# A DiT block on one core: LN2's second token tile turned by VectorE and moved by DMA, ten fc1 tiles per small token tile, two weight blocks loaded earlier, a P V remainder in quarters

## The chip, the core and the metric

The kernel runs on one core of one Trainium2 chip. The metric is the device time in microseconds. Before the change it is 241.34 us (median of 3 runs, 241.32 to 241.39). A core has TensorE (matrix multiplication into PSUM), VectorE, ScalarE (activation functions, copies), GpSimd and SyncE (which here only issues DMAs); each runs its own instructions strictly in order, and they wait for each other on semaphores.

## The reference

One block of a diffusion transformer: B = 2, N = 256 tokens, D = 1152, 2 heads of 576, hidden width F = 4608, all inputs bfloat16.

```python
mod = (_silu(c) @ w_mod).reshape(B, 6, 1, D)
shift_a, scale_a, gate_a, shift_m, scale_m, gate_m = [mod[:, i] for i in range(6)]
h = _layernorm(x) * (1 + scale_a) + shift_a
qkv = (h @ wqkv).reshape(B, N, 3, H, Dh)
...
attn = _softmax(einsum('bqhd,bkhd->bhqk', q, k) * Dh ** (-0.5))
a = einsum('bhqk,bkhd->bqhd', attn, v).reshape(B, N, D) @ wo
x = x + gate_a * a
h2 = _layernorm(x) * (1 + scale_m) + shift_m
return x + gate_m * (_gelu(h2 @ w_fc1) @ w_fc2)
```

## The kernel before

The 512 tokens are four tiles of 128 (t = 0 to 3; two tiles per batch element b = t // 2). D is nine chunks of 128 (kt), F is 36 tiles of 128 (f). Weights live in SBUF regions that are used again and again; all of SBUF is one tensor, `arena`, all of PSUM one tensor, `psum`, so these two names stand in nearly every line of the profile.

The kernel is written as a list of units (one operation each, or a group of matmuls). TensorE and SyncE run theirs in the order of the program text. For the other engines a planner orders the units by the length of what hangs on them, with a cost for each unit; `S.in_order` (lines 1317 to 1333) fixes the order of the units that it names. Waits are worked out from the memory that units read and write. PSUM has eight banks; `acc_bank()` hands out those in `acc` in turn.

What matters here begins with the attention output, P V: `pv(b, h)` makes eight chunks of 128 features; the 128 features left over (64 of each head, since 576 = 4 x 128 + 64) are made by `pv_halves()` (line 1127), two matmuls of 64 columns side by side in the array (`tile_position`), four such pairs. Just ahead of it, `rows()` makes the modulation vectors with matmuls that have 2 columns of weights, four side by side.

Then `wo_tile(t)` (line 1161) for t = 0 to 3: three PSUM tiles of 384 features, nine matmuls each. For each one VectorE multiplies by the gate (`wo_t1`, line 1173), GpSimd adds x (`wo_x1`, line 1174); then LN2's statistics on VectorE (`bn_ln2`, `aggr`, `veps`, lines 751 to 754), rstd and the negative mean times rstd on GpSimd (`rstd`, `negm2`, `nmr2`), and the normalized tile on ScalarE (`xn2_t`, line 1180).

fc1 needs the normalized tile transposed (features in partitions). Two ways are in the kernel:

- `xn2_T(t)`, used for t = 1, inside `wo_tile(3)` after its first third: nine transposes on TensorE (line 706), then nine scalings out of PSUM (`h2T_1_kt`: four on VectorE, five on ScalarE).
- `xn2_turn(t)` (one VectorE transpose of 32 x 32 blocks, `h2turn_t`, line 1206) with `xn2_move(t)` (four DMAs from SBUF to SBUF on SyncE's queue, `mv_h2_t_a`, which put the blocks in their partitions; then nine scalings in place, `h2T_t_kt`, lines 1216 on ScalarE and 1219 on VectorE), used for t = 0, 2, 3. `TURNED` says where the turned tile is put before it is moved.

fc1 follows (`fc1_tile(f, tok0, ntok)`): nine matmuls for each f and token range, then a GELU on ScalarE (line 1229) into `GT[f]`. w_fc1 comes in nine blocks of four f each (`wfc1_load(q)`, 1152 KB), into four buffers; blocks 0 and 1 are loaded during attention, 2 and 3 into the region of wv and w_mod's shift part, behind tile 0's moves on SyncE's queue. The order of fc1: f = 0 to 4 on tile 1, f = 0 to 4 on tile 0, f = 5 to 14 on tiles 0 and 1 together (256 tokens), f = 0 to 14 on tiles 2 and 3, then f = 15 to 35 on all 512 tokens. During that, `ld_gm` brings the last part of w_mod (2592 KB), from which VectorE works out the MLP's gate (`mlp_gate`), and SyncE loads w_fc1's and w_fc2's other blocks. fc2 ends the kernel.

SyncE's order in this part: blocks 0 and 1, the second gate (`ld_g1`), tile 0's moves, blocks 2 and 3, the moves of tiles 2 and 3, `ld_gm`, then blocks 4 to 8 of w_fc1 and the four of w_fc2.

Of the kernel before, what the change touches and what calls it, by code (L numbers as in the profile page):

```python
# [508 lines left out]
KT = 9  # L509
# [4 lines left out]
SCALE = DH ** -0.5  # L514
CH = 384
NCH = 3
F0 = 15
KC = 5
KG = 6
NG = 9  # L520
# [3 lines left out]
def c_mm(n):  # L524
    return max(n / 2.4 + 2.5, 27.0)
# [26 lines left out]
def build_kernel(nc, x, c, wqkv, wo, w_mod, w_fc1, w_fc2, out):  # L552
# [5 lines left out]
    with (  # L558
# [14 lines left out]
        def ps16(bank, c0=0, n=1024):  # L573
            v = psum[:, bank * 512: (bank + 1) * 512].bitcast(BF16)
            return v[:, c0:c0 + n]
# [111 lines left out]
        def dve(cost, fn, reads, writes, name):  # L687
            return S.op("dve", cost, fn, reads=reads, writes=writes, name=name)

        def act(cost, fn, reads, writes, name):  # L690
            return S.op("act", cost, fn, reads=reads, writes=writes, name=name)
# [10 lines left out]
        def mm(o, l, r, st, sp, **kw):  # L702
            S.instr(lambda e: e.matmul(o, lhsT=l, rhs=r, start=st, stop=sp, **kw), reads=[l, r], writes=[o])  # L703

        def tr(o, i_, idn):
            S.instr(lambda e: e.transpose(o, i_, idn), reads=[i_, idn], writes=[o])  # L706
# [420 lines left out]
        def pv_halves():  # L1127
            S.unit("pe", 4 * c_mm(256) + 100.0, "PV_halves")
            for b in range(2):
                for kjt in range(2):  # L1130
                    for h in range(2):
                        f0 = 512 + 64 * h
                        mm(psum[64 * h:64 * h + 64, b * 256:b * 256 + 256], V[:, 2 * b + kjt, f0:f0 + 64],
                           PTS[b * 2 + h][:, kjt], b == 0 and kjt == 0, b == 1 and kjt == 1, skip_group_check=True,
                           tile_position=(0, 64 * h))
            copy_on("act", OT[:, 4, :], ps32(0), 512, False, "OT_ev_4")

        def pv(b, h):
# [11 lines left out]
                copy_on(eng, OT[:, g:g + 2, tok], src, 512, False, "OT_ev%d_%d" % (b, g))  # L1150

        act(1500, lambda e: e.activation(out=SUMS[:, 0:1], in_=NHALF, func=ACTF.Gelu_apprx_tanh), [NHALF], [SUMS[:, 0:1]], "gelu_tab")
        acc = [2, 3, 4, 6, 5, 7]
        acc_rr = [0]

        def acc_bank():
# [1 line left out]
            acc_rr[0] += 1  # L1158
            return b

        def wo_tile(t, before={}):
            b = t // 2
            for ci in range(NCH):
                if ci in before:
                    before[ci]()
                S.unit("pe", KT * c_mm(CH), "wo_%d_%d" % (t, ci))
                o = ps32(acc_bank(), 0, CH)
                for g in range(KT):
                    mm(o, OT[:, g, t * 128:(t + 1) * 128], WO[:, g, ci * CH:(ci + 1) * CH], g == 0, g == KT - 1)
                ga = GA[b][:, ci * CH:(ci + 1) * CH]  # L1170
                x1c = X1[:, t, ci * CH:(ci + 1) * CH]
                xs = X[:, t, ci * CH:(ci + 1) * CH]
                dve(550, lambda e, o=o, ga=ga, x1c=x1c: e.tensor_tensor(out=x1c, in0=o, in1=ga, op=ALU.mult), [o, ga], [x1c], "wo_t1_%d_%d" % (t, ci))  # L1173
                S.op("pool", 930, lambda e, xs=xs, x1c=x1c: e.tensor_tensor(out=x1c, in0=x1c, in1=xs, op=ALU.add),  # L1174
                     reads=[x1c, xs], writes=[x1c], name="wo_x1_%d_%d" % (t, ci))
            rs, nm, m, xn2, x1 = RSTD2[:, t:t + 1], NMR2[:, t:t + 1], MV2[:, t, 0:1], XN2[t], X1[:, t, :]
            ln_stats_dve(x1, [X1[:, t, ci * CH:(ci + 1) * CH] for ci in range(NCH)], BN2[:, t, :], MV2[:, t, :], rs, "ln2_%d" % t)
            pool(200, lambda e: e.tensor_scalar(out=nm, in0=m, scalar1=-1.0, scalar2=None, op0=ALU.mult), [m], [nm], "negm2_%d" % t)
            pool(200, lambda e: e.tensor_tensor(out=nm, in0=nm, in1=rs, op=ALU.mult), [nm, rs], [nm], "nmr2_%d" % t)  # L1179
            act(1344, lambda e: e.activation(out=xn2, in_=x1, func=ACTF.Identity, scale=rs, bias=nm), [x1, rs, nm], [xn2], "xn2_%d" % t)  # L1180

        last_h2T = [None]

        def xn2_T(t):
            b = t // 2
            xn2 = XN2[t]
            S.unit("pe", KT * c_mm(128), "xn2T_%d" % t)
            hi, lo = ((7, 6), (1, 0))[t % 2]
            slot = [ps16(hi, kt * 128, 128) if kt < 4 else ps16(lo, (kt - 4) * 128, 128) for kt in range(KT)]
            for kt in range(KT):  # L1190
                tr(slot[kt], xn2[:, kt * 128:(kt + 1) * 128], IDENT)
            for kt in range(KT):
                o, dst = slot[kt].rearrange("p (g i) -> p g i", i=32), H2T[:, kt, 4 * t:4 * t + 4, :]
                s1, s2 = SC1M[:, kt * 2 + b:kt * 2 + b + 1], SHM[:, kt * 32 + b:kt * 32 + b + 1]
                if kt < 4:
                    last_h2T[0] = dve(335, lambda e, o=o, dst=dst, s1=s1, s2=s2: e.tensor_scalar(out=dst, in0=o, scalar1=s1, scalar2=s2, op0=ALU.mult, op1=ALU.add),
                        [o, s1, s2], [dst], "h2T_%d_%d" % (t, kt))
                else:
                    act(440, lambda e, o=o, dst=dst, s1=s1, s2=s2: e.activation(out=dst, in_=o, func=ACTF.Identity, scale=s1, bias=s2),
                        [o, s1, s2], [dst], "h2T_%d_%d" % (t, kt))  # L1200

        TURNED = {0: H2F[3], 2: XN2[0], 3: XN2[1]}

        def xn2_turn(t):
            src, flat = XN2[t].rearrange("p (k x c) -> p c k x", k=KT, c=4), TURNED[t]
# [2 lines left out]
        def xn2_move(t):  # L1208
            b, b0 = t // 2, 0
            for a in range(4):  # L1210
                dma(H2F[t][:, 288 * a:288 * a + 288], TURNED[t][32 * a:32 * a + 32, :], P * 576, "mv_h2_%d_%d" % (t, a), run=576)
            for kt in range(KT):
                dst = H2T[:, kt, 4 * t:4 * t + 4, :]
                s1, s2 = SC1M[:, kt * 2 + b:kt * 2 + b + 1], SHM[:, kt * 32 + b:kt * 32 + b + 1]
                if kt % 3 if t == 0 else kt % 3 == 2:
                    act(330, lambda e, dst=dst, s1=s1, s2=s2: e.activation(out=dst, in_=dst, func=ACTF.Identity, scale=s1, bias=s2),  # L1216
                        [dst, s1, s2], [dst], "h2T_%d_%d" % (t, kt))
                    continue
                last_h2T[0] = dve(220, lambda e, dst=dst, s1=s1, s2=s2: e.tensor_scalar(out=dst, in0=dst, scalar1=s1, scalar2=s2, op0=ALU.mult, op1=ALU.add),  # L1219
                    [dst, s1, s2], [dst], "h2T_%d_%d" % (t, kt))  # L1220
# [46 lines left out]
        def wfc2_load(q):  # L1267
            dma(WFC2[:, 9 * q:9 * q + 9, :], wfc2_v[:, 9 * q:9 * q + 9, :], 9 * P * D * 2, "ld_wfc2_%d" % q, run=2304)

        wo_tile(0)  # L1270
        xn2_turn(0)
        xn2_move(0)
        wfc1_load(2)
        wfc1_load(3)
        wo_tile(1)
        wo_tile(2)
        xn2_turn(2)
        wo_tile(3, {1: lambda: xn2_T(1)})
        xn2_turn(3)
        xn2_move(2)  # L1280
        xn2_move(3)
        dma(WGM, wmod_v[:, :, 5 * D:6 * D], D * D * 2, "ld_gm", run=2304)
        for tok0 in (128, 0):
            for f in range(0, 5):
                fc1_tile(f, tok0, 128)
        for f in range(5, F0):
            fc1_tile(f, 0, 256)
        mlp_gate(last_h2T[0])
        for f in range(F0):
# [11 lines left out]
        for t in range(4):  # L1301
# [4 lines left out]
            for (c0, c1) in pieces:  # L1306
# [3 lines left out]
                for j in range(JT):  # L1310
# [13 lines left out]
        S.in_order("act", ["sexp_0_0", "sexp_0_1", "qk_ev8", "spn_0_0", "spn_0_1", "v_ev0_0", "sexp_2_0", "sexp_2_1", "sexp_1_0", "sexp_1_1", "v_ev0_1",  # L1324
                           "spn_2_0", "spn_2_1", "spn_1_0", "spn_1_1", "v_ev0_2", "sexp_3_0", "sexp_3_1", "v_ev1_0", "spn_3_0", "spn_3_1", "v_ev1_1", "v_ev1_2"])
        S.in_order("act", ["OT_ev0_0", "OT_ev0_2", "OT_ev1_0", "OT_ev1_2", "OT_ev_4", "OT_ev0_5", "OT_ev1_5", "gelu_tab", "xn2_0"])
        S.in_order("pool", ["wo_x1_0_0", "wo_x1_0_1", "wo_x1_0_2", "wo_x1_1_0", "rstd_ln2_0", "nmr2_0", "wo_x1_1_1", "wo_x1_1_2", "wo_x1_2_0", "rstd_ln2_1", "nmr2_1", "wo_x1_2_1", "wo_x1_2_2",
                            "wo_x1_3_0", "rstd_ln2_2", "nmr2_2", "wo_x1_3_1", "wo_x1_3_2", "rstd_ln2_3"])
        S.in_order("dve", ["wo_t1_0_0", "wo_t1_0_1", "bn_ln2_0_0", "wo_t1_0_2", "bn_ln2_0_1", "wo_t1_1_0", "bn_ln2_0_2", "aggr_ln2_0", "veps_ln2_0", "wo_t1_1_1",
                           "bn_ln2_1_0", "wo_t1_1_2", "bn_ln2_1_1", "wo_t1_2_0", "bn_ln2_1_2", "aggr_ln2_1", "veps_ln2_1", "h2turn_0", "wo_t1_2_1", "bn_ln2_2_0", "wo_t1_2_2", "bn_ln2_2_1",  # L1330
                           "wo_t1_3_0", "h2T_1_0", "h2T_1_1", "h2T_1_2", "h2T_1_3", "bn_ln2_2_2", "aggr_ln2_2", "veps_ln2_2", "wo_t1_3_1", "wo_t1_3_2", "h2T_0_0", "h2T_0_3", "h2T_0_6",
                           "bn_ln2_3_0", "bn_ln2_3_1", "bn_ln2_3_2", "aggr_ln2_3", "veps_ln2_3", "h2turn_2", "h2turn_3"])
        S.in_order("act", ["xn2_0", "xn2_1", "h2T_1_4", "h2T_1_5", "h2T_1_6", "h2T_1_7", "h2T_1_8", "h2T_0_1", "h2T_0_2", "h2T_0_4", "h2T_0_5", "h2T_0_7", "h2T_0_8", "gelu_0_128", "xn2_2"])
        S.schedule()
        if VERBOSE:
            S.report()
# [50 lines left out]
```

## Time and profile before

| | |
|---|---|
| time, median of 3 runs | 241.34 us |
| time of the profiled execution | 241.23 us |
| its span | 239.3 us |
| granted TensorE clock | 0.999 |
| VectorE busy, share of the span | 52% |
| ScalarE | 31% |
| GpSimd | 10% |
| DMA, mean over the span | 222 GB/s, 53.01 MB |
| first wo tile's read on VectorE starts | 79.53 us |
| last wo tile's read on VectorE starts | 96.13 us |
| first GELU | 97.76 us |
| last GELU ends | 167.10 us |

Times inside the execution are counted from the start of its span. "Busy" is the time in which an engine had at least one instruction running; instructions of one engine overlap a little, so the lengths of a group add up to more than its busy time. Matmul ends are modelled. Lines are those of the kernel before, printed above; a helper's line stands for all that it issues (703 for every matmul, 706 for every transpose on TensorE, 684 for every DMA).

### The profile page before, as it was taken

The page shows a single profiled execution, that of the slowest core. Times are in us where ns is not written, and L with a number is a line of the kernel's source. Part 1 is how long each engine was busy: PE and PEld are TensorE (multiplying, and loading weights), DVE is VectorE, ACT ScalarE, POOL GpSimd, SP SyncE. Part 2 cuts the span into 40 slices and gives each one's busy share as a digit, 9 for nine tenths or more (in the row PEclk, how much of TensorE's full clock was granted, in tenths as well). Part 3 has the DMA queues.
Part 4 walks back from the last instruction along what each step waited for, and adds up shares of the span by engine and source line. Part 5 has one row for each costly group of instructions (what it writes and reads, how often), then busy time and mean ns, then how long its engine had stood idle before and what let it go on. Part 6 is the DMA issues. An engine that isn't in the chain of part 4 may idle for free.

```text
span 239.3 us, 4153 instructions
## 1 busy us (share of the span) xinstructions
PE 234.0 (98%) x1752; PEld 148.2 (62%) x1755; DVE 124.4 (52%) x230; ACT 73.2 (31%) x158; POOL 23.5 (10%) x48
## 2 busy tenths in 40 slices
PE   6999999999999999999999999999999999999995
PEld 2687844466667666988884444444666656666664
DVE  2654389979997689943199997000111111111112
ACT  4940540458535325956332333322000000000000
POOL 1300000000201486500000001100000000000000
PEclk9999999999999999999999999999999999999999
DMA  6999999999799302948999999992000000000000
GB/s 223 366 377 392 389 391 391 395 414 401 237 358 356 104 0 59 346 118 292 340 346 385 372 373 386 369 391 82 0 19 16 16 19 16 16 17 25 24 19 19
DMA packets 34397, 53.01 MB, mean 222 GB/s; under 512 B 4107, under 2 KB 19851, under 8 KB 34379
## 3 DMA queue, kind: packets, MB, share of 16 engines
q1 hardware_dynamic: 33776, 51.85, 61.8%
q0 software_dynamic: 432, 0.89, 1.0%
q8 instruction: 14, 0.23, 0.4%
q10 hardware_dynamic: 171, 0.01, 0.0%
q14 instruction: 4, 0.03, 0.0%
HBM read 50.15 MB, written 1.19 MB: 215 GB/s over the span
## 4 chain that ended last, share of the span: by engine, by line
PE 91%; DMA 5%; SPq 3%; issue 0%; DVE 0%
PE psum L703 90%; DMA arena<-in_w_mod_dram 5%; SPq L684 3%; PE psum L706 0%; DVE arena L1314 0%; DVE arena L1315 0%
## 5 line engine op out<-in xcount | busy, mean ns | idle before, releaser
L703 PE MATMUL psum<-arena 128*128 128x384 bf16 (+8 forms) x1706 | 231.9, 304 | 2.4 <-POOL arena L729 1.5
L703 PEld LDWEIGHTS psum<-arena 128*128 128x128 bf16 (+1 forms) x1709 | 145.6, 97 | 86.7 <-issue 4.2
L1314 DVE TENSOR_TENSOR arena<-psum,arena 128x384 f32<-128x384 f32 (+2 forms) x13 | 6.9, 527 | 74.8 <-PE psum L703 74.8
L1229 ACT ACTIVATE arena<-psum 128x256 bf16<-128x256 f32 (+2 forms) x56 | 23.8, 442 | 39.3 <-PE psum L703 39.3
L698 ACT ACTIVATE arena<-psum 128x512 bf16<-128x512 f32 (+5 forms) x35 | 18.6, 561 | 31.3 <-PE psum L703 31.3
L1067 DVE SCALAR_TENSOR_TENSOR arena<-arena 128x1152 f32<-128x1152 bf16 x16 | 22.5, 1411 | 0.2
L1102 DVE SCALAR_TENSOR_TENSOR arena<-arena 128x1152 f32<-128x1152 bf16 x16 | 21.3, 1408 | 0.0
L684 POOL DMA_DIRECT2D dit_scratch<-arena x6 | 3.5, 583 | 101.4 <-DVE arena L1084 53.9
L751 DVE BATCH_NORM_STATS2 arena<-arena 128x6 f32<-128x384 f32 (+1 forms) x18 | 9.5, 549 | 4.3 <-DMA arena<-in_x_dram 4.2
L1174 POOL TENSOR_TENSOR arena<-arena 128x384 f32<-128x384 f32 x12 | 10.9, 912 | 6.4 <-DVE arena L1173 6.3
L1180 ACT ACTIVATE arena<-arena 128x1152 bf16<-128x1152 f32 x4 | 5.4, 1344 | 9.4 <-POOL arena L1179 9.4
L1173 DVE TENSOR_TENSOR arena<-psum,arena 128x384 f32<-128x384 f32 x12 | 6.6, 550 | 2.9 <-PE psum L703 2.9
L700 DVE CAST arena<-psum 128x512 bf16<-128x512 f32 x8 | 5.4, 684 | 4.5 <-PE psum L703 4.5
L1315 DVE TENSOR_TENSOR arena<-arena 128x384 bf16<-128x384 f32 (+2 forms) x13 | 6.9, 527 | 0.5
L1219 DVE TENSOR_SCALAR arena<-arena 128x128 bf16<-128x128 bf16 x15 | 4.7, 379 | 3.8 <-DMA arena<-arena 3.8
L1216 ACT ACTIVATE arena<-arena 128x128 bf16<-128x128 bf16 x12 | 5.0, 482 | 2.1 <-DMA arena<-arena 2.1
L1099 DVE TENSOR_SCALAR arena<-arena 128x1152 f32<-128x1152 bf16 x2 | 1.5, 816 | 7.8 <-DMA arena<-in_w_mod_dram 7.8
L1206 DVE STREAM_TRANSPOSE arena<-arena 128x1152 bf16<-128x1152 bf16 x3 | 4.1, 1372 | 1.1 <-ACT arena L1180 1.1
L1018 ACT ACTIVATE arena<-psum,arena 128x256 bf16<-128x256 f32 x8 | 3.7, 469 | 2.4 <-DVE arena L1015 1.9
L706 PEld LDWEIGHTS psum<-arena 128*128 128x128 bf16 (+1 forms) x46 | 2.9, 98 | 1.7 <-DMA arena<-in_c_dram 1.3
L706 PE MATMUL psum<-arena 128*128 128x128 bf16 (+1 forms) x46 | 3.5, 218 | 0.4 <-DMA arena<-in_c_dram 0.4
L755 POOL TENSOR_TENSOR arena<-arena 128x1 f32<-128x1 f32 x6 | 3.4, 567 | 3.9 <-DVE arena L754 3.7
(66 smaller groups left out, 66.6 us busy)
## 6 DMA issues: line engine op xcount, KB each, us to landing
arena<-in_w_fc_dram SPq DMA_DIRECT2D x9, 1152.0 KB, 8.9
arena<-in_w_fc_dram SPq DMA_DIRECT2D x4, 2592.0 KB, 19.6
arena<-in_wqkv_dram SPq DMA_DIRECT2D x18, 288.0 KB, 10.3
arena<-in_w_mod_dram SPq DMA_DIRECT2D x6, 864.0 KB, 12.9
arena<-in_w_mod_dram SPq DMA_DIRECT2D x3, 1728.0 KB, 20.2
arena<-in_wqkv_dram SPq DMA_DIRECT2D x1, 2592.0 KB, 18.0
arena<-in_wo_dram SPq DMA_DIRECT2D x1, 2592.0 KB, 9.7
arena<-in_w_mod_dram SPq DMA_DIRECT2D x1, 2592.0 KB, 11.0
```

The source lines that it names most:

```text
L684: return S.op(eng, 500.0 if eng == "sp" else 150.0, lambda e: e.dma_start(dst, src), reads=[src], writes=[dst], name=name, dma_bytes=nbyte ...
L698: act(c_act(n), lambda e: e.activation(out=dst, in_=src, func=ACTF.Copy), [src], [dst], name)
L703: S.instr(lambda e: e.matmul(o, lhsT=l, rhs=r, start=st, stop=sp, **kw), reads=[l, r], writes=[o])
L706: S.instr(lambda e: e.transpose(o, i_, idn), reads=[i_, idn], writes=[o])
L751: dve(550, lambda e, s=s, o=o: e.bn_stats(out=o, in_=s), [s], [o], "bn_%s_%d" % (tag, ci))
L1067: ga_units[(b, kt)] = dve(150 + FG * 1.1, lambda e, o=o, w=w, s1=s1: e.scalar_tensor_tensor(out=o, in0=w, scalar=s1, in1=o, op0=ALU.mult, ...
L1102: u = dve(1300, lambda e, o=o, w=w, s1=s1: e.scalar_tensor_tensor(out=o, in0=w, scalar=s1, in1=o, op0=ALU.mult, op1=ALU.add), [w, s1, o], ...
L1173: dve(550, lambda e, o=o, ga=ga, x1c=x1c: e.tensor_tensor(out=x1c, in0=o, in1=ga, op=ALU.mult), [o, ga], [x1c], "wo_t1_%d_%d" % (t, ci))
L1174: S.op("pool", 930, lambda e, xs=xs, x1c=x1c: e.tensor_tensor(out=x1c, in0=x1c, in1=xs, op=ALU.add), reads=[x1c, xs], writes=[x1c], name=" ...
L1229: act(c_act(ntok), lambda e: e.activation(out=dst, in_=o, func=ACTF.Gelu_apprx_tanh), [o], [dst], "gelu_%d_%d" % (f, tok0))
L1314: dve(c_dve_psum32(w), lambda e, o=o, gm=gm, t1=t1: e.tensor_tensor(out=t1, in0=o, in1=gm, op=ALU.mult), [o, gm], [t1], "fc2_t1_%d_%d" % ( ...
L1315: dve(c_dve_32(w), lambda e, t1=t1, x1c=x1c, ost=ost: e.tensor_tensor(out=ost, in0=t1, in1=x1c, op=ALU.add), [t1, x1c], [ost], "fc2_out_%d ...
```

## The change

- P V's remainder: in place of two matmuls of 64 columns side by side, four of 32 columns.
- The accumulator banks are eight in place of six.
- `xn2_T` goes. Tile 1 is turned by VectorE and moved by four DMAs like the others; its turned form is put into the place of H2F[2].
- Blocks 2 and 3 of w_fc1 are issued ahead of all the moves.
- fc1's order: f = 0 to 9 on tile 0, f = 0 to 9 on tile 1, f = 10 to 15 on both, f = 0 to 15 on tiles 2 and 3, f = 16 to 35 on all tokens (`F0` is 16 in place of 15).
- The scalings are shared out anew between VectorE and ScalarE (tile 0: four and five; tile 1: six and three), and the fixed orders of GpSimd, VectorE and ScalarE are written anew.

```diff
-F0 = 15
+F0 = 16
...
-                    for h in range(2):
-                        f0 = 512 + 64 * h
-                        mm(psum[64 * h:64 * h + 64, b * 256:b * 256 + 256], V[:, 2 * b + kjt, f0:f0 + 64],
-                           PTS[b * 2 + h][:, kjt], b == 0 and kjt == 0, b == 1 and kjt == 1, skip_group_check=True,
-                           tile_position=(0, 64 * h))
+                    for q in range(4):
+                        r = slice(32 * q, 32 * q + 32)
+                        mm(psum[r, b * 256:b * 256 + 256], V[:, 2 * b + kjt, 512 + 32 * q:544 + 32 * q],
+                           PTS[b * 2 + q // 2][:, kjt], b == 0 and kjt == 0, b == 1 and kjt == 1, skip_group_check=True,
+                           tile_position=(0, 32 * q))
...
-        acc = [2, 3, 4, 6, 5, 7]
+        acc = [2, 3, 4, 6, 5, 7, 0, 1]
...
-        def xn2_T(t):
...
-        TURNED = {0: H2F[3], 2: XN2[0], 3: XN2[1]}
+        TURNED = {0: H2F[3], 1: H2F[2], 2: XN2[0], 3: XN2[1]}
...
-                if kt % 3 if t == 0 else kt % 3 == 2:
+                if (kt % 2 or kt == 8) if t == 0 else kt > 5 if t == 1 else kt % 3 == 2:
                     act(330, ...
...
+        wfc1_load(2)
+        wfc1_load(3)
         wo_tile(0)
         xn2_turn(0)
         xn2_move(0)
-        wfc1_load(2)
-        wfc1_load(3)
         wo_tile(1)
+        xn2_turn(1)
+        xn2_move(1)
         wo_tile(2)
         xn2_turn(2)
-        wo_tile(3, {1: lambda: xn2_T(1)})
+        wo_tile(3)
         xn2_turn(3)
...
-        for tok0 in (128, 0):
-            for f in range(0, 5):
+        for tok0 in (0, 128):
+            for f in range(0, 10):
                 fc1_tile(f, tok0, 128)
-        for f in range(5, F0):
+        for f in range(10, F0):
             fc1_tile(f, 0, 256)
```

VectorE's new order from the second tile on, and ScalarE's:

```diff
+        S.in_order("dve", [... 'wo_t1_1_2', 'bn_ln2_1_1', 'h2turn_0', 'bn_ln2_1_2', 'aggr_ln2_1', 'veps_ln2_1', 'wo_t1_2_0', 'wo_t1_2_1', 'wo_t1_2_2', 'bn_ln2_2_0',
+            'h2turn_1', 'h2T_0_0', 'h2T_0_2', 'h2T_0_4', 'h2T_0_6', 'wo_t1_3_0', 'bn_ln2_2_1', 'bn_ln2_2_2', 'aggr_ln2_2', 'veps_ln2_2', 'wo_t1_3_1', 'wo_t1_3_2',
+            'h2T_1_0', 'h2T_1_1', 'h2T_1_2', 'h2T_1_3', 'h2T_1_4', 'h2T_1_5', 'bn_ln2_3_0', 'bn_ln2_3_1', 'bn_ln2_3_2', 'aggr_ln2_3', 'veps_ln2_3', 'h2turn_2', 'h2turn_3'])
+        S.in_order("act", ['xn2_0', 'xn2_1', 'h2T_0_1', 'h2T_0_3', 'h2T_0_5', 'h2T_0_7', 'h2T_0_8', 'gelu_0_0', ... 'gelu_5_0', 'h2T_1_6', 'h2T_1_7', 'h2T_1_8', 'xn2_2'])
```

The planner sets gelu_6_0 to gelu_9_0 between and behind tile 1's three scalings on ScalarE, ahead of xn2_2.

More of the change, by code (lines that the diff above doesn't have):

```diff
@@ L1159, in acc_bank, with wo_tile @@
             return b
-        def wo_tile(t, before={}):
+        def wo_tile(t):
             b = t // 2
             for ci in range(NCH):
-                if ci in before:
-                    before[ci]()
                 S.unit("pe", KT * c_mm(CH), "wo_%d_%d" % (t, ci))
@@ L1182, in build_kernel @@
         last_h2T = [None]
-        def xn2_T(t):
[L1185 to L1200, printed above, removed]
-        TURNED = {0: H2F[3], 2: XN2[0], 3: XN2[1]}
+        TURNED = {0: H2F[3], 1: H2F[2], 2: XN2[0], 3: XN2[1]}
         def xn2_turn(t):
@@ L1326, in build_kernel @@
         S.in_order("act", ["OT_ev0_0", "OT_ev0_2", "OT_ev1_0", "OT_ev1_2", "OT_ev_4", "OT_ev0_5", "OT_ev1_5", "gelu_tab", "xn2_0"])
-        S.in_order("pool", ["wo_x1_0_0", "wo_x1_0_1", "wo_x1_0_2", "wo_x1_1_0", "rstd_ln2_0", "nmr2_0", "wo_x1_1_1", "wo_x1_1_2", "wo_x1_2_0", "rstd_ln2_1", "nmr2_1", "wo_x1_2_1", "wo_x1_2_2",
+        S.in_order("pool", ["wo_x1_0_0", "wo_x1_0_1", "wo_x1_0_2", "wo_x1_1_0", "rstd_ln2_0", "nmr2_0", "wo_x1_1_1", "wo_x1_1_2", "rstd_ln2_1", "nmr2_1", "wo_x1_2_0", "wo_x1_2_1", "wo_x1_2_2",
                             "wo_x1_3_0", "rstd_ln2_2", "nmr2_2", "wo_x1_3_1", "wo_x1_3_2", "rstd_ln2_3"])
[L1329 to L1333, printed above, removed]
+        S.in_order("dve", ['wo_t1_0_0', 'wo_t1_0_1', 'bn_ln2_0_0', 'wo_t1_0_2', 'bn_ln2_0_1', 'wo_t1_1_0', 'bn_ln2_0_2', 'aggr_ln2_0', 'veps_ln2_0', 'wo_t1_1_1', 'bn_ln2_1_0', 'wo_t1_1_2', 'bn_ln2_1_1', 'h2turn_0', 'bn_ln2_1_2', 'aggr_ln2_1', 'veps_ln2_1', 'wo_t1_2_0', 'wo_t1_2_1', 'wo_t1_2_2', 'bn_ln2_2_0', 'h2turn_1', 'h2T_0_0', 'h2T_0_2', 'h2T_0_4', 'h2T_0_6', 'wo_t1_3_0', 'bn_ln2_2_1', 'bn_ln2_2_2', 'aggr_ln2_2', 'veps_ln2_2', 'wo_t1_3_1', 'wo_t1_3_2', 'h2T_1_0', 'h2T_1_1', 'h2T_1_2', 'h2T_1_3', 'h2T_1_4', 'h2T_1_5', 'bn_ln2_3_0', 'bn_ln2_3_1', 'bn_ln2_3_2', 'aggr_ln2_3', 'veps_ln2_3', 'h2turn_2', 'h2turn_3'])
+        S.in_order("act", ['xn2_0', 'xn2_1', 'h2T_0_1', 'h2T_0_3', 'h2T_0_5', 'h2T_0_7', 'h2T_0_8', 'gelu_0_0', 'gelu_1_0', 'gelu_2_0', 'gelu_3_0', 'gelu_4_0', 'gelu_5_0', 'h2T_1_6', 'h2T_1_7', 'h2T_1_8', 'xn2_2'])
         S.schedule()
```

## The prediction

> **What bounds the kernel now.** I read the page's busy table first, then the chain of waits in order of time, then ScalarE's, VectorE's and SyncE's timelines between 78 and 130 us, then the busy table cut into half-microsecond stretches for the DMA.
>
> ```profile
> PE 234.0 (98%) x1752; PEld 148.2 (62%) x1755; DVE 124.4 (52%) x230; ACT 73.2 (31%) x158; POOL 23.5 (10%) x48
> ...
> 50.16 42.50 PE psum L703 x339
> 92.66 0.50 PE psum L706 x9
> 93.16 143.61 PE psum L703 x990
> 236.77 0.02 issue
> ```
>
> From 50.16 to 236.77 the chain is TensorE alone (start, length): no wait of any other engine is in it. So the edit is worth what it takes from TensorE's own work, less any stall that it creates. The nine L706 matmuls are tile 1's transposes, inside the chain.
>
> VectorE's timeline (first line) and ScalarE's (start, length, engine, line, operation, in brackets the wait before it and who ended it):
>
> ```profile
> 96.13 0.56 DVE L1173 TENSOR_TENSOR arena<-psum,arena 128x384 f32<-128x384 f32 x1 [0.15 <-PE psum L703]
> ...
> 104.10 0.38 ACT L1229 ACTIVATE arena<-psum 128x256 bf16<-128x256 f32 x1 [0.60 <-PE psum L703]
> 105.08 0.38 ACT L1229 ACTIVATE arena<-psum 128x256 bf16<-128x256 f32 x1 [0.60 <-PE psum L703]
> ...
> 111.96 0.38 ACT L1229 ACTIVATE arena<-psum 128x256 bf16<-128x256 f32 x1 [0.60 <-PE psum L703]
> ...
> 125.71 0.38 ACT L1229 ACTIVATE arena<-psum 128x256 bf16<-128x256 f32 x1 [0.60 <-PE psum L703]
> 127.65 0.60 ACT L1229 ACTIVATE arena<-psum 128x512 bf16<-128x512 f32 x1 [1.56 <-PE psum L703]
> ...
> 166.50 0.60 ACT L1229 ACTIVATE arena<-psum 128x512 bf16<-128x512 f32 x1 [1.34 <-PE psum L703]
> ```
>
> These are readers that wait for TensorE, so their starts clock its tiles: 96.13 is the end of the last wo tile, each GELU the end of an fc1 tile, 111.96 that of the first tile on tokens 256 and up.
>
> **TensorE's work, term by term.** A 256-token fc1 tile takes (125.71 - 111.96) / 14 = 0.982 us; a 512-token tile (166.50 - 127.65) / 20 = 1.943. Between 96.13 and 111.96 lie ten 128-token tiles and eleven of 256, so a 128-token tile takes (15.83 - 11 x 0.982) / 10 = 0.503. Before: 10, 25 and 21 tiles of the three sizes: 5.03 + 24.55 + 40.80 = 70.38 us. After: 20, 22 and 20: 10.06 + 21.60 + 38.86 = 70.52. Splitting costs **+0.14 us**: two small tiles are hardly dearer than one of double width.
>
> The transposes go: 0.50 in the chain; the same from VectorE's twelve wo reads, which start at 79.53 and, three pitches later, at 83.92 (pitch 1.463): 96.13 - 79.53 - 11 x 1.463 = 0.507. **-0.51 us.**
>
> P V's remainder: eight matmuls with 64 columns become sixteen with 32.
>
> The weight loads' timeline:
>
> ```profile
> 73.25 2.06 PEld L703 LDWEIGHTS psum<-arena 128*2 128x2 bf16 x72 [0.21 <-issue]
> 75.55 0.36 PEld L703 LDWEIGHTS psum<-arena 128*64 128x64 bf16 x8 [0.25 <-issue]
> 76.11 3.97 PEld L703 LDWEIGHTS psum<-arena 128*128 128x128 bf16 x31 [0.20 <-issue]
> ```
>
> The halves take 75.55 to 76.11: 0.56 for four steps of two. The row vectors before them already run as four tiles side by side: 72 matmuls of 288 in 2.30 us, 0.128 a step of four; for 256 columns 0.114, four steps 0.455. The weight loads pause 0.25 before and 0.20 behind the halves. With the quarters both neighbours ahead are quads, so the first pause should shrink. Lower end: 0.455 and no first pause, 0.56 + 0.10 - 0.455 = 0.20 gained. Upper end: each quarter takes as long as one half does now, 16 x 0.07 = 1.12, 0.56 lost. The nearest row is the quads', though with 2 columns of weights; I take **-0.10**.
>
> The Trainium skill (TensorEngine Tiling (Array Packing), Key Properties) says that a change of tiling mode drains the array, a change of tile within it does not; the two pauses agree, and by it the sum would be 0.1 better than without. Its Restrictions say that column tiling turns the fast weight load off, which speaks against four more loads per step; halves and quads are both column-tiled already, and no run here shows a 32-column load.
>
> Sum: +0.14 - 0.51 - 0.10 = **-0.47 us**. The profiled execution took 241.23 (span 239.3); so 240.76, and beside the median 241.34, which is 0.11 higher, **240.87**.
>
> **What must hide, and by how much.** VectorE, ScalarE, GpSimd and SyncE do the rest. TensorE now leaves wo at 96.08 - 0.51 = 95.57 and asks for tile 0 at once (its ninth chunk at 95.57 + 8 x 0.056 = 96.02), for tile 1 ten small tiles later, at 100.60, for tiles 2 and 3 at 100.60 + 5.03 + 6 x 0.982 = 111.52, a chunk every 0.109.
>
> ScalarE's and VectorE's scalings of the turned tiles before (each ends its wait for the moves):
>
> ```profile
> 95.44 2.42 ACT L1216 ACTIVATE arena<-arena 128x128 bf16<-128x128 bf16 x6 [0.38 <-DMA arena<-arena]
> ...
> 96.60 1.84 DVE L1219 TENSOR_SCALAR arena<-arena 128x128 bf16<-128x128 bf16 x3
> ...
> 109.27 1.43 DVE L1219 TENSOR_SCALAR arena<-arena 128x128 bf16<-128x128 bf16 x6 [1.24 <-DMA arena<-arena]
> ```
>
> SyncE's issues (arena from arena are the moves):
>
> ```profile
> 91.15 2.50 SPq L684 DMA_DIRECT2D arena<-arena  x4
> 93.69 1.32 SPq L684 DMA_DIRECT2D arena<-in_w_fc_dram  x2
> ...
> 102.19 1.42 SPq L684 DMA_DIRECT2D arena<-arena  x1
> ```
>
> Tile 0: xn2_0 ends at 87.91 (as before); the turn now comes straight behind bn_1_1, 87.95 to 89.32 (1.37). Before, the turn ended at 91.08 and the four moves had landed at 95.40, 4.3 later; so 93.65. ScalarE's five scalings (2.42 for six: 0.39 apart, 0.48 the last) end at 95.7, VectorE's four (1.43 for six: 0.24 each) at 94.9. Slack 0.3.
>
> Tile 1: the early turn pushes tile 1's statistics and the wo reads of tile 2 back by 0.4, against a slack of two wo tiles in the banks. xn2_1 ends near 92.4, the turn at 93.8, the moves land at 98.0. Its six VectorE scalings meet GpSimd's last two adds (0.91 each, 97.3 to 99.2). Before, the three scalings at 96.60 took 1.84 instead of 0.72, and ended only behind two adds at 96.38 to 98.17; so here they end near 100.3, not 99.5. The sixth chunk is asked at 100.88. ScalarE's three, between GELUs, end at 100.4; the ninth chunk is asked at 101.05.
>
> Tiles 2 and 3: bn_3 waits behind those scalings; three statistics (1.47), aggregate and epsilon end near 102.0, 1.7 later than the 100.28 of before. GpSimd's rstd, xn2_3 and turn_3 follow: 104.07 + 1.7 = 105.8. SyncE is busy with tile 2's moves (from 103.7, 0.64 each) till 106.2, so tile 3's last is issued at 108.1 and lands at 110.4; scalings from 110.4 to 111.85 (chunk 0 at 110.75, chunk 7 last; asked at 111.52 and 112.28). Slack 0.4; before it was near 1.
>
> The early loads pass all the moves on SyncE. They are issued behind the gate load at 81.2; their bytes start 2.3 us after issue and take 6.4 (96.0 to 102.4 in the half-microsecond table), so they are gone at about 90.2, while the first moves' bytes start at 91. They fill a stretch (84 to 90) with no traffic. The w_mod load behind the moves goes out 1.2 later (107.53 to 108.75) and shifts the stream that runs without a gap from 117.2 to 162.7 by at most that. Its last piece is asked for at 166.1, the last fc1 block at 158.3 and is in by 155.5: hidden, unless the shift passes 2.5 us. Eight accumulator banks instead of six cost nothing; the GELUs that wait behind xn2_2 and xn2_3 have four us of banks in front of them.
>
> **Rivals.**
> 1. *Tile 0's moves stand behind the early blocks.* For: in a loaded queue the 16 P moves landed in 7.1 us (median), against 2.2 for the h2 moves. Against: 84 to 90 is empty now, and the blocks should be out by 90.2. At 7.1 tile 0 is 4.9 late: 4.9 - 0.3 = 4.6 us of stall at fc1's start; wo_t1_3_0 is queued behind VectorE's four waiting scalings, and tile 2's statistics behind that. From 1.3 us late on it is slower than before (0.3 of slack, 0.47 of gain, 0.5 to be seen). One to two us late: 241.6 to 242.6; in full 245.5.
> 2. *A move or a link in tile 3's chain is late.* One of the twelve moves took 1.42 to issue instead of 0.6 (102.19). Such a one among tile 0's, 2's or 3's moves costs 0.8 less the slack: 0.4 to 0.5, 241.3; among tile 1's it is hidden. For: 0.3 to 0.4 is all the slack there is, on a sum over some twenty links. Against: every link is shown above.
> 3. *The quarters do not run four abreast:* +0.56 in place of -0.10: 241.5. Against: the quads of the row vectors do.
> 4. *More is gained:* both pauses around the quarters go, and the small tiles lose less: 0.2 more, 240.65.
> 5. *The diff does nothing for time* because what leaves TensorE is made up by waits: that is 2 in its whole length, 241.3.
>
> **How the numbers follow.** The forecast (no stall, 240.87 give or take 0.15) 0.45; rival 1 0.13; rivals 2 and 5 0.24; rival 3 0.06; rival 4 0.12. 0.2% is 0.48 us, about what a measurement here tells from nothing: faster means below 240.86, which cuts the forecast in two. Faster: 0.23 of it and all of rival 4, with a little of 2: 0.37. Slower (above 241.82): most of rival 1 and tails of 2 and 3, 0.19. Same: 0.44. The range goes from rival 4's lower edge, 240.55, into rival 1, 242.0; the forecast's own is 240.7 to 241.05.
>
> **What would show it.** Right: the chain from 50 us on is still TensorE alone, with no L706 piece near 92; the GELU that closes the first tile on tokens 256 comes at 112.45 (111.96 + ten more small tiles, 5.03, - four tiles of 256, 3.93, - 0.61); loads behind the row vectors with no 0.25 pause. Wrong: a TensorE wait on ScalarE or VectorE near 96 (rival 1), 101 or 111.5 (rival 2), or on a weight DMA behind 155; quarters longer than 0.56.

## The result, and the profile after

The changed kernel took 242.94 us (median of 4 runs, 242.55 to 243.31), the kernel before 241.33 beside it: ratio 1.0067, 95% interval 1.0047 to 1.0087. It is slower by 1.6 us where 0.47 less was forecast, and outside the range (240.55 to 242.0). Measured again in two later series, beside the kernel before each time, the ratio was 1.0008 (0.9994 to 1.0022) and 1.0043 (1.0024 to 1.0061): the change costs between nothing and 0.7%, and does not gain. The profiled execution took 242.67, its span 240.7.

The page's busy table and the chain of waits of the changed kernel (start, length, what); before, the chain from 50 us on was TensorE alone:

```profile
PE 234.7 (98%) x1805; PEld 149.0 (62%) x1808; DVE 126.6 (53%) x234; ACT 73.2 (30%) x161; POOL 23.3 (10%) x48
...
50.38 39.63 PE psum L703 x330
...
91.38 2.81 DMA arena<-arena
...
94.30 2.04 ACT arena L1196 x5
...
96.38 4.77 PE psum L703 x82
...
101.45 1.24 ACT arena L1178
...
102.72 1.39 DVE arena L1186
...
106.65 1.53 SPq L684
...
109.47 0.42 issue
109.90 2.40 DMA arena<-arena
...
112.80 125.39 PE psum L703 x792
```

TensorE leaves the chain twice. At 96.38 it has waited for ScalarE's scalings of tile 0, which waited for tile 0's moves. At 112.80 it has waited for VectorE's scalings of tile 3, and behind these stand the four moves, SyncE's issues, the turn of tile 2 and xn2_2. Who TensorE waited for, in the view of waits (total, times, longest):

```profile
PE psum L703 <- DVE arena L1199: 0.7, 1, 0.7
...
PE psum L703 <- ACT arena L1196: 0.2, 1, 0.2
```

These 0.9 us are too few, since a matmul's modelled length covers the first part of a pause, and a tile whose chunks arrive one by one crawls without a pause. The GELUs clock it better (ScalarE's timeline):

```profile
96.65 0.28 ACT L1209 ACTIVATE arena<-psum 128x128 bf16<-128x128 f32 x1 [0.32 <-PE psum L703]
...
113.57 1.15 ACT L1209 ACTIVATE arena<-psum 128x256 bf16<-128x256 f32 x3
115.32 0.38 ACT L1209 ACTIVATE arena<-psum 128x256 bf16<-128x256 f32 x1 [0.60 <-PE psum L703]
...
129.07 0.38 ACT L1209 ACTIVATE arena<-psum 128x256 bf16<-128x256 f32 x1 [0.60 <-PE psum L703]
...
167.92 0.60 ACT L1209 ACTIVATE arena<-psum 128x512 bf16<-128x512 f32 x1 [1.35 <-PE psum L703]
```

A 256-token tile still takes (129.07 - 115.32) / 14 = 0.982, and the tile that closes at 115.32 is the second on tokens 256: the first closed near 114.34, where the prediction had 112.45.

Executions differ by more than 1 us before the wo stage begins, so I measure all traces from the start of the first wo read on VectorE (79.53 before, 79.64 after). To the first GELU, the sum of the prediction gives 11 x 1.463 + 0.50 = 16.59; to the last GELU's start it gives before's 86.97 less 0.37 = 86.60. After: 17.01 (96.65 - 79.64) and 88.28 (167.92 - 79.64). So 0.42 us is lost at the hand-over of tile 0 and 88.28 - 86.60 - 0.42 = 1.26 at that of tile 3, 1.68 in all; less the 0.37 that the sum gives, 1.31 behind the first wo read (end: 159.09 after it, before 157.78).

### The profile page after: what moved, and what is told of

Read it like the earlier page. It is cut to its first block, busy times and chain, and to the rows that moved or that the text cites. A ratio compares the mean times of both kernels' runs of the same rounds, so it can differ in the third digit from the quotient of the medians.

```text
span 240.7 us, 4274 instructions
## 1 busy us (share of the span) xinstructions
PE 234.7 (98%) x1805; PEld 149.0 (62%) x1808; DVE 126.6 (53%) x234; ACT 73.2 (30%) x161; POOL 23.3 (10%) x48
## 4 chain that ended last, share of the span: by engine, by line
PE 82%; DMA 10%; SPq 4%; ACT 1%; DVE 1%; issue 1%; DVEq 0%; ACTq 0%
PE psum L703 82%; DMA arena<-in_wqkv_dram 8%; SPq L684 4%; DMA arena<-arena 2%; ACT arena L1196 1%; DVE arena L1186 1%; ACT arena L1178 1%; PE psum L706 0%; DVE arena L1199 0%; ACT arena L1209 0%; DVE arena L1296 0%; DVE arena L1297 0%; DVEq L479 0%; ACTq L479 0%
## 5 line engine op out<-in xcount | busy, mean ns | idle before, releaser
L703 PE MATMUL psum<-arena 128*128 128x384 bf16 (+10 forms) x1768 | 233.0, 300 | 3.2 <-POOL arena L729 1.5
L703 PEld LDWEIGHTS psum<-arena 128*128 128x128 bf16 (+3 forms) x1771 | 146.9, 97 | 87.5 <-issue 3.9
L1209 ACT ACTIVATE arena<-psum 128x256 bf16<-128x256 f32 (+2 forms) x62 | 24.9, 416 | 39.3 <-PE psum L703 39.1
L1067 DVE SCALAR_TENSOR_TENSOR arena<-arena 128x1152 f32<-128x1152 bf16 x16 | 22.5, 1412 | 0.2
L1199 DVE TENSOR_SCALAR arena<-arena 128x128 bf16<-128x128 bf16 x22 | 6.4, 357 | 5.1 <-DMA arena<-arena 5.1
L1196 ACT ACTIVATE arena<-arena 128x128 bf16<-128x128 bf16 x14 | 6.0, 484 | 3.7 <-DMA arena<-arena 3.7
L1186 DVE STREAM_TRANSPOSE arena<-arena 128x1152 bf16<-128x1152 bf16 x4 | 5.5, 1378 | 1.0 <-ACT arena L1178 0.8
L1023 ACT ACTIVATE arena<-arena 128x256 bf16<-128x256 bf16 x8 | 3.6, 502 | 0.2 <-DVE arena L1020 0.2
L1014 DVE TENSOR_REDUCE arena<-psum 128x2 f32<-128x512 f32 x4 | 2.8, 690 | 1.2 <-PE psum L703 1.1
```

The lines of the kernel that those rows point to most:

```text
L1067: ga_units[(b, kt)] = dve(150 + FG * 1.1, lambda e, o=o, w=w, s1=s1: e.scalar_tensor_tensor(out=o, in0=w, scalar=s1, in1=o, op0=ALU.mult, ...
L1186: dve(c_dve_32(D), lambda e: e.transpose(flat, src), [src], [flat], "h2turn_%d" % t)
L1209: act(c_act(ntok), lambda e: e.activation(out=dst, in_=o, func=ACTF.Gelu_apprx_tanh), [o], [dst], "gelu_%d_%d" % (f, tok0))
```

## The experiments

Ten more runs, each with a profile and measured beside the kernel before. Diffs are against the changed kernel where nothing else is said.

| kernel | median us | beside before's | ratio, 95% | first wo read to first / last GELU |
|---|---|---|---|---|
| before | | | | - / 86.97 |
| the sum | | | | 16.59 / 86.60 |
| changed, first trace | 242.94 | 241.33 | 1.0047 to 1.0087 | 17.01 / 88.28 |
| after_again | 241.48 | 241.40 | 0.9994 to 1.0022 | 16.59 / 87.43 |
| after_third | 242.29 | 241.21 | 1.0024 to 1.0061 | 16.59 / 87.62 |
| pv_quarters | 241.24 | 241.12 | 0.9983 to 1.0018 | - / 86.97 |
| no_moves_0_3 | 241.40 | 241.12 | 0.9997 to 1.0038 | 16.60 / 87.11 |
| loads_before_gate | 241.70 | 241.12 | 1.0007 to 1.0041 | 16.59 / 87.93 |
| move3_on_act | 248.38 | 241.12 | 1.0271 to 1.0316 | 16.85 / 93.02 |
| fetch_shifted | 242.62 | 241.40 | 1.0020 to 1.0064 | 16.59 / 86.88 |
| move3_act_held | 241.12 | 241.40 | 0.9978 to 1.0010 | 16.59 / 86.60 |
| all_three | 241.01 | 241.40 | 0.9967 to 0.9999 | 16.59 / 86.73 |
| early_and_held | 241.15 | 241.21 | 0.9987 to 1.0027 | 16.59 / 86.90 |

**pv_quarters**: in the kernel before, only `pv_halves` is exchanged for the quarters.

> The kernel before with the P V quarters alone. If four tiles of 32 columns run abreast, as the profile after suggests (weight loads from the row vectors to the end of the quarters 2.74 us, before 2.86): 0.10 to 0.12 less than before, 241.2. If the quarters were dearer and something else hid it: 241.4 to 241.9.

The ratio is 1.000 (0.9983 to 1.0018), too coarse for 0.1 us. The traces tell it: the weight loads from the row vectors on, changed kernel:

```profile
73.47 2.53 PEld L703 LDWEIGHTS psum<-arena 128*2 128x2 bf16 x88 [0.21 <-issue]
76.21 19.88 PEld L703 LDWEIGHTS psum<-arena 128*128 128x128 bf16 x132 [0.21 <-issue]
```

72 loads of the row vectors and 16 of the quarters run in one piece; the pause of 0.25 ahead of the halves is gone, that of 0.21 behind them is left. 2.74 us against 2.86: 0.12 gained. In pv_quarters, from the start of the chain's piece of 49 matmuls at 41 us to the end it is 195.88 us (41.10 to 236.98), before 196.01 (41.30 to 237.31): 0.13.

**no_moves_0_3**

```diff
-            for a in range(4):
+            for a in range(4 if t in (1, 2) else 0):
```

> The changed kernel without the moves of tiles 0 and 3 (eight of sixteen DMAs left out; their scalings then work on what lies there). Theory: TensorE's own work was counted rightly, and the whole loss is two hand-overs, tile 0 (0.4 us) and tile 3 (1.4): without these moves 240.87, give or take 0.15, and no TensorE wait in the chain behind 50 us. Rival: TensorE's work itself is dearer than the sum (twenty small tiles, eight banks): 241.5 or more.

Without these moves two tiles are scaled from whatever lies in their places, so only the time is of use. It took 241.40, not 240.87. The traced execution reached the wo stage 1.1 us late, its granted clock being 0.57 between 11 and 15 us, and leaving the moves out made a loss of its own: tile 3's scalings, which now wait for no move, were ordered between VectorE's other work and held tile 1 up. The first GELU is in time (16.60), the fourteenth small tile is not: its GELU starts at 104.30, the sum has 80.67 + 16.59 + 13 x 0.503 = 103.80. With these 0.50 off, 87.11 - 0.50 = 86.61: the sum to 0.01. The cleaner proof is move3_act_held, below.

**loads_before_gate**

```diff
         gate_store(1)
-        gate_load(1)
         v_proj(0, 2)
         for t in range(1, 4):
             for ci in range(NCH):
                 v_proj(t, ci)
+        wfc1_load(2)
+        wfc1_load(3)
+        gate_load(1)
...
-        wfc1_load(2)
-        wfc1_load(3)
         wo_tile(0)
```

> The changed kernel with fc1's blocks 2 and 3 issued ahead of the second gate load, which waits for its stores until 81 us, so that their bytes are out before tile 0's moves. Theory: the tail of these blocks costs tile 0's moves 0.6 us: TensorE's wait near 96 goes (0.4), and the chain to tile 3 is 0.5 earlier: 242.0 to 242.2. Rival: the moves are slow by themselves, or tile 3's chain does not hang on tile 0's: 242.5 to 242.9.

Tile 0 is in time (16.59). In the changed kernel's first trace the early blocks had not landed when tile 0's moves came; the busy table in half microseconds (stretch, length, clock, DMA share, GB/s):

```profile
83.50:84.00 0.50, 1.00 0.50 110
...
90.00:90.50 0.50, 1.00 1.12 354
90.50:91.00 0.50, 1.00 1.01 297
91.00:91.50 0.50, 1.00 0.74 222
```

The blocks' bytes start slowly beside the gate load (110 GB/s at 83.5) and run at about 300 GB/s until 91; the second block lands at 93.39, and the moves, issued from 89.49 on, land behind it from 93.59 to 94.19, 14.6 after the first wo read, against 14.1 in the prediction. It is so in all six traces that have the loads in this place and tile 0's moves behind them: the first move lands 0.2 after the second block. Tile 0's loss follows that block. It is 0.42 where the block lands 13.75 after the first wo read, 0.26 at 13.59 (move3_on_act), and nothing at 13.06 to 13.31.

With the blocks gone first, the first move lands 2.1 after its issue in place of 4.1, and the last one at 92.95 (13.9). The time can't show what that is worth: 1.0024 lies among the changed kernel's own three ratios. Tile 3 is as late as before (87.93 - 86.60 = 1.33), since TensorE asks for it 0.42 earlier too, while its moves still queue, here behind an issue of 1.67.

**move3_on_act**

```diff
-                dma(H2F[t][:, ...], TURNED[t][...], P * 576, "mv_h2_%d_%d" % (t, a), run=576)
+                dma(H2F[t][:, ...], TURNED[t][...], P * 576, "mv_h2_%d_%d" % (t, a), run=576, eng="act" if t == 3 else "sp")
...
-        S.n_other_dma_sems = 12
+        S.n_other_dma_sems = 16
```

> The changed kernel with tile 3's four moves issued on ScalarE's queue in place of SyncE's. Theory: behind VectorE's turn at 106.3 it is SyncE's queue (tile 2's moves until 106.6, one issue of 1.53 us, a gap of 0.4) that makes tile 3 late; freed of it, its moves land 1.2 us earlier: 241.6 to 242.0. Rival: the turn itself is what is late, and the queue costs only its 0.3: 242.5 to 242.9.

The expectation was wrong: 248.38 us, 7 more than before. With the four moves off SyncE's queue, nothing held the w_mod load behind them. The chain:

```profile
105.77 0.28 ACT arena L1209
106.05 0.56 ACTq L684
...
107.98 7.29 DMA arena<-arena
115.28 0.03 issue
115.30 0.05 DVEq L479
...
115.77 48.59 PE psum L703 x288
```

The last move was issued at 107.98 and took 7.3 us to land in place of 2.3, because 2592 KB went out from 106.22 on. TensorE's wait was 4.1 us, and behind it the granted clock fell (stretch, length, clock, DMA share, GB/s):

```profile
115.00:119.00 4.00, 0.59 0.25 99
119.00:123.00 4.00, 0.99 0.10 16
```

That takes 4 x 0.41 + 4 x 0.01 = 1.7 us more. The long landing of rival 1 came by another door, and it cost more than the wait alone.

**move3_act_held**: the same, and the load waits for the moves.

```diff
         dma(WGM, wmod_v[:, :, 5 * D:6 * D], D * D * 2, "ld_gm", run=2304)
+        moved = [u.instrs[0] for u in S.units if u.name.startswith("mv_h2_3_")]
+        S.units[-1].instrs[0].deps.update(moved)
```

> The changed kernel with tile 3's four moves on ScalarE's queue, and the last w_mod load held until they have landed (in move3_on_act it went ahead of them and they landed 7.3 us after issue). Theory: SyncE's queue made tile 3 late by 1.3 to 1.7 us (tile 2's moves, the long issue, the gap): moves issued from 106.3 to 108.9 land at 110.7 in place of 112.3, and 0.9 to 1.3 of the 1.4 lost there comes back: 1.0 us less than the changed kernel. Rival: the moves are slow on their way, not in the queue: at most 0.3 less.

VectorE's turn of tile 3 and its scalings (VectorE's timeline):

```profile
104.14 1.38 DVE L1186 STREAM_TRANSPOSE arena<-arena 128x1152 bf16<-128x1152 bf16 x1 [0.85 <-ACT arena L1178]
...
109.95 1.43 DVE L1199 TENSOR_SCALAR arena<-arena 128x128 bf16<-128x128 bf16 x6 [0.38 <-DMA arena<-arena]
```

The scalings start 4.4 after the turn's end (after_again, same series: turn from 104.09, scalings at 111.13, 5.7 after its end). TensorE is the chain from 16.57 to 236.22 without a break, and the first wo read to the last GELU is 86.60, the sum to the hundredth. Against after_again 0.83 is won in the trace, 0.36 in the medians, whose intervals overlap.

**after_again** and **after_third**: the changed kernel itself.

> The changed kernel itself, once more, as the measure for the other kernels of this call and for a second trace. If what made tile 3 late belongs to the program, the trace again has a TensorE wait of about 0.7 us near 112, an issue of 1.4 to 1.7 us on SyncE right behind the fetch of 16 KB of instructions near 106, and a gap of 0.4 before the last move; the ratio to before is 1.005 to 1.009. If it was chance: no long issue, and a ratio near 1.003.

> The changed kernel a third time. The two traces so far lose 0.42 and 0.00 us at tile 0 and 1.26 and 0.83 at tile 3 (time from the first wo read to the last GELU, less the sum). Theory: both losses are arrivals that hang on transfers and on the length of one issue, so they differ from execution to execution: 0 to 0.5 at tile 0, 0.7 to 1.4 at tile 3, ratio to before 1.000 to 1.007. Against it: a loss at tile 3 under 0.3.

Both lose nothing at tile 0, and 0.83 and 1.02 at tile 3. The long issue (1.21, 1.34) and the gap (0.43 and 0.43) are there each time. The traced execution of after_third is the fastest of its twelve (241.20 beside a median of 242.29, all at a full clock); what the slower ones lose besides, no trace shows. SyncE's moves of tile 3 and the load behind them in the first trace:

```profile
106.65 1.53 SPq L684 DMA_DIRECT2D arena<-arena  x1
108.22 0.61 SPq L684 DMA_DIRECT2D arena<-arena  x1
108.87 0.60 SPq L684 DMA_DIRECT2D arena<-arena  x1
109.90 0.54 SPq L684 DMA_DIRECT2D arena<-arena  x1
110.49 0.73 SPq L684 DMA_DIRECT2D arena<-in_w_mod_dram  x1
```

**fetch_shifted**

```diff
         warm(5, "b")
+        S.unit("pe", 60 * 27.0, "fill")
+        for i in range(60):
+            mm(ps32(2, 0, 2), IDENT, Q4B[:, 0:2], True, True)
```

> The changed kernel with 60 matmuls of 2 columns (120 TensorE instructions, no result of theirs is used) more in the stretch at the start in which TensorE waits for the first weights. Theory: the long issue on SyncE comes from the fetch of TensorE's instructions (one in some 256 instructions, 7.2 us apart among the small tiles, where they were 18 us apart before); 120 more move the fetches of 99.1 and 106.35 forward by 3.3 us, to 95.8 and 103.0: the long issue is then among tile 1's moves (95.9), and tile 3's first move takes 0.6 again and lands 0.9 earlier; less what tile 1's pays (0.3), 0.4 to 0.8 less than the changed kernel, if the filling hides at the start. Rival: the long issue belongs to SyncE's own queue: it stays with tile 3's first move, and the time stays.

The fetch of instructions stands in the view of the DMA queues (queue, packets, MB, share of 16 engines); after_again between 105.65 and 105.70, then this run between 103.85 and 103.90:

```profile
q8 instruction: 1, 0.02, 133.6%
...
q8 instruction: 1, 0.02, 116.5%
```

So it came 22.9 after the first wo read, where after_again has 26.45: 3.5 earlier (expected 3.3), before tile 2's first move at 105.01. All sixteen moves then took 0.54 to 0.60; tile 3's first two:

```profile
107.53 0.60 SPq L684 DMA_DIRECT2D arena<-arena  x1
108.17 0.60 SPq L684 DMA_DIRECT2D arena<-arena  x1
```

To the last GELU it is 86.88, 0.55 less than after_again. The expected long issue among tile 1's moves did not come: a fetch was there at 95.00, tile 1's first move was issued 0.37 behind it and took 0.54. The whole time is 1.1 more, and the first wo read is at 80.94, after_again's at 79.20. The clock accounts for that in this trace:

```profile
8.00:12.00 4.00, 0.57 1.04 382
```

4 x 0.43 = 1.7 us go there. Six of this kernel's eleven executions have a mean clock of 0.993 or less, of after_again's twelve none; that the filling brings it about is likely, not shown. The gap of 0.43 ahead of the last move stayed (109.42 to 109.84).

**all_three** and **early_and_held**: loads_before_gate with move3_act_held; all_three also has

```diff
-'h2T_1_0', 'h2T_1_1', ... 'h2T_1_5', 'bn_ln2_3_0', 'bn_ln2_3_1', 'bn_ln2_3_2',
+'bn_ln2_3_0', 'h2T_1_0', 'bn_ln2_3_1', 'h2T_1_1', ... 'h2T_1_5', 'bn_ln2_3_2',
```

> The changed kernel with the early loads ahead of the second gate load, tile 3's moves on ScalarE's queue with the w_mod load held behind them, and LN2's statistics of tile 3 set between tile 1's scalings while GpSimd's adds lock these out (bn_ln2_3_0, one scaling, bn_ln2_3_1, five scalings, bn_ln2_3_2). Theory: both hand-overs are in time, no TensorE wait behind 50 us, and the sum of the prediction holds: 0.4 to 0.5 us less than before (ratio 0.998). Rival: some other wait takes their place: as before or more.

> The changed kernel with the early loads ahead of the gate load and tile 3's moves on ScalarE's queue, w_mod's load held; VectorE's order as in the changed kernel. Theory: no wait at either hand-over; first wo read to last GELU 86.60 us, as the sum has it; ratio to before 0.997 to 0.999. Rival: all_three's 0.13 (86.73) and its wait of 0.2 for a w_fc2 block come again, from the loads' new place rather than from the statistics' order.

all_three has the lowest median: 241.01 beside 241.40, ratio 0.9983 (0.9967 to 0.9999), just clear of the kernel before. It doesn't reach the sum. To the last GELU it is 86.73; 0.11 of the 0.13 is lost by the first 512-token GELU (49.80, by the sum 49.69), since tile 2's last move landed 3.75 us after its issue and VectorE's scalings of both tiles came late in one row. From the last GELU to the end it is 71.15 where the kernel before has 70.81; TensorE waits for a w_fc2 block at 166.

early_and_held is in time up to its first 512-token GELU (49.69), loses 0.30 till the last one, at a w_fc1 block near 160, and 0.33 behind it, where TensorE again waits for w_fc2. Of its expectation's rival, the wait for w_fc2 came without the new order of the statistics; all_three's 0.13 was another loss. That the loads' new place causes the wait is not shown: move3_act_held, with the old place, has no such wait, but single traces of each are all there is.

What the new order of the statistics is worth stays open too, as the intervals of 0.9983 and 1.0007 overlap. It ended the statistics 0.92 earlier (epsilon at 100.68 against 101.60), but the turn of tile 2 then waited for xn2_2, which stands behind tile 1's scalings on ScalarE, and started at 101.85 as before; only tile 3's turn ended 0.5 earlier.

## Why the prediction was wrong

**TensorE's sum: right.** +0.14 for the split and -0.51 for the transposes came out together, at 86.60 in move3_act_held, exactly; the quarters at -0.12 for -0.10, with the first pause gone and the second left. The Trainium skill's rule (TensorEngine Tiling (Array Packing), Key Properties), by which only a change of mode drains the array, agrees with that.

**The bound of the first move: near in number, wrong in mechanism.** Tile 0's moves were to land 14.1 after the first wo read (93.65); they landed at 14.6 in the first trace and at 14.0 in the other two. But the early blocks were said to be gone "at about 90.2", before the moves' first bytes. The second block landed at 93.39, 92.44 and 92.00, and the moves behind it each time. A loss begins where the block lands at 13.75 - 0.42 = 13.33 after the first wo read; 13.24 and 13.12 in the later two traces are in time by luck. Price 0.42, once in three traces.

**Tile 3: here it failed.** The step reads "SyncE is busy with tile 2's moves (from 103.7, 0.64 each) till 106.2, so tile 3's last is issued at 108.1 and lands at 110.4 ... Slack 0.4". Behind the first wo read, in us:

| | predicted | after_again | first trace |
|---|---|---|---|
| tile 1's scalings end (VectorE) | 20.8 | 20.7 | 21.1 |
| tile 3's epsilon ends | 22.5 | 22.6 | 23.0 |
| tile 3's turn ends | 26.3 | 26.3 | 26.7 |
| its first move is issued | 26.7 | 26.6 | 27.0 |
| its last move is issued | 28.6 | 29.5 | 30.3 |
| its scalings start | 30.9 | 31.9 | 32.8 |
| lost at tile 3 | 0 | 0.83 | 1.26 |

Everything up to SyncE's queue is right to 0.1 us in after_again. In the queue, the first move takes 1.21 (or 1.53) in place of 0.60, and SyncE stands still for 0.43 before the last. A lateness of 1.0 cost 0.83, so the slack was 0.2, not 0.4. In the first trace everything is 0.4 later from tile 0's late moves on, because the scalings that wait for them stand ahead of wo_t1_3_0 and of tile 2's statistics in VectorE's order; but TensorE asks for tile 3 by so much later too. What differs from trace to trace is the long issue and the last move's landing:

| | length of the first move's issue | last move, issue to landing | lost at tile 3 |
|---|---|---|---|
| fetch_shifted | 0.60 | 2.35 | 0.28 |
| after_again | 1.21 | 2.28 | 0.83 |
| after_third | 1.34 | 2.35 | 1.02 |
| first trace | 1.53 | 2.40 | 1.26 |
| loads_before_gate | 1.67 | 2.32 | 1.33 |

Add what each has more than after_again in the two middle columns to 0.83, and the last column comes out to 0.01. The 0.28 that is left without a long issue is about the gap of 0.43 less the slack of 0.2.

The long issue was in view: the profile before has one of 1.42 at 102.19. The prediction took it for one in twelve, put 0.4 to 0.5 us on it, and added it to a rival with a chance of 0.24. It is not chance here. In all three traces of the changed kernel, in the kernel before and in four variants, the issue on SyncE that begins with a fetch of 16 KB of instructions, or up to 0.34 behind it, is the long one (before: fetch at 102.14, issue at 102.19; after: 106.37 and 106.65), and with the fetch moved ahead of tile 2's moves it was gone. A fetch alone doesn't do it, as tile 1's moves in fetch_shifted show. What was mis-sized is rival 2: its link is late in all three traces, by 0.6 to 0.9, and a second one by 0.43, on a slack of 0.2.

**The early loads' other end: right, with no room.** The w_mod load was to be hidden "unless the shift passes 2.5 us". In the first trace it went out 2.9 later than before, counted from the first wo read, without a TensorE wait, but there TensorE itself was 1.7 late. In move3_act_held, all_three and early_and_held, where TensorE came nearly in time, it went out 2.7 to 2.9 later, and the stretch from the first 512-token GELU to the end was 0.1, 0.4 and 0.6 longer. So this bound is about where it was put.

**Rivals.** Rival 1's queue was real in every trace with the early loads in their place, at a price of 0 to 0.42; its full landing came only in move3_on_act, behind another load (7.3 us, where 7.1 had been put on it). Rivals 3 and 4 fell: the quarters ran abreast, and the second pause stayed. Rival 5 is what after_again's median shows (241.48 beside 241.40), by way of rival 2.

## What to carry to other kernels

A sum over the engine that bounds the kernel can be right to a hundredth and decide nothing, when the change moves work to engines whose cover is thinner than the gain: here 0.47 us of gain stood on 0.2 us of slack. For such a hand-over, add up the queue that issues its transfers, one issue at a time, and put one disturbed issue of the profile into the sum, not into a rival. A transfer that is taken off a queue releases what was queued behind it; hold that back, or it takes the bandwidth first.

## What the runs showed of the hardware that was not expected

The 16 KB fetches follow TensorE's instructions. There are 14 in the changed kernel's 3613 matmuls and weight loads, one in 258 in the mean, and 120 more instructions at the start (fetch_shifted) brought the one at 26.45 after the first wo read forward by 3.5 us (120 x 0.028 = 3.4). They are 7.2 us apart among the small tiles (99.13, 106.37), which run at 0.028 us an instruction, and were 11.4 apart among the 256-token tiles before (102.14, 113.55). So small tiles bring them more often.

On SyncE, the issue that began between 0.02 us ahead of such a fetch and 0.34 behind it took 1.07 to 1.67 us in place of 0.6, among the moves and the load behind them, in eight traces. Two issues as near took no longer than others: tile 1's first move in fetch_shifted (0.54, begun 0.37 behind the fetch) and a w_fc2 load in move3_on_act (0.50, begun at 126.25, 0.13 behind). In the eight, moves issued shortly before were still on their way; in these two none was. Whether that is the condition was not tried. On ScalarE's queue the long issue came once (1.26, fetch at 106.24, issue at 106.33). It did not come three times: issues of 0.68, 0.63 and 0.63, begun 0.08 and 0.04 ahead of the fetch and 0.02 behind it. How a fetch lengthens an issue, the runs don't show.

The still stand of 0.43 before the sixteenth move came in all five traces that have sixteen moves on SyncE, with and without a long issue, and ended each time 0.14 to 0.16 after tile 3's first move had landed. On ScalarE's queue the fourth move didn't wait for that (move3_act_held: issued at 107.62, first landing at 108.23). Its cause is open.
